# An attention and mixture-of-depths kernel: loads of k, q and v issued later, and row sums begun one turn later

## The chip, the cores and the metric

The kernel runs on one core of a Trainium2 chip. The metric is the device time of one execution in microseconds (us); of several runs of a kernel the median is given. The profile shows one execution. Its engines are PE (TensorE; PEld is its weight load), DVE (VectorE), ACT (ScalarE), POOL (GpSimd) and SP (SyncE, which here only issues transfers). "L370" is line 370 of the kernel before.

## The reference

q, k and v are 8 batches x 8 heads x 576 positions x 64, phi is 8 x 8 x 576 x 32.

```python
a = exp(phi - max(phi, axis=2)); a = a / (sum(a, axis=2) + 1e-9)   # over the 576 positions
k_m = einsum('bhsm,bhsd->bhmd', a, k)
v_m = einsum('bhsm,bhsd->bhmd', a, v)
attn = softmax(q @ k_m.T / 8)                                     # over the 32 columns
x = (attn @ v_m) with the heads side by side                      # 8 x 576 x 512
scores = x @ w_gate
for each batch: of the 128 positions with the highest scores
    out = x + sigmoid(score) * (relu(x @ w1) @ w2)                # w1 512 x 1024
all other positions: out = x
```

## The kernel before

The sequence of the work is written by hand: the kernel is a set of Python generators, and a main loop takes some steps of each in every **turn**. What a generator issues between two of its `yield`s stands together in the programs of the engines, and each engine then runs its own program in that order.

**Softmax groups.** `softmaxes` works on 16 groups (a batch and half of its heads, 128 rows by 576). A group takes eleven turns; its arithmetic is on DVE and ACT (L192 to L275; L275 is the last DVE step, in which e is finished). For the first eight groups two channels are used in alternation, for groups 8 to 15 one. `group` loads the next group's phi (L98) and its own k (L102). At its end `keys` transposes e on PE (L315), copies it with ACT (L317), splits it into a high and a low part on DVE (L321, L323), stores these parts in DRAM through POOL (`aparts`, L326), and multiplies with k on PE (L332), from which ACT makes `kbd` (L337). k has one buffer in each channel, phi has two.

**v.** `split_v` runs in every second turn while both channels live: it loads v (L284, two buffers), splits it on DVE (L294, L296) and stores both parts in DRAM through POOL (`vparts`, L299). A buffer can be loaded again when its store has landed.

**Sums.** `values` sums a x v for a set of two batches (four groups). Rows of `vparts` and `aparts` come back in 32 chunks: SP issues one transfer of 288 KB (L349) and four of 36 KB (L356) for a chunk, two chunks ahead, into three buffers, so that a load waits until PE has read the chunk three before it. PE multiplies a chunk with 72 small matmuls (L370), with a yield after each eighth. `all_sums` starts a set when its four groups are made and five more turns have passed; `steps()` says how many steps of the sums a turn takes (7 while softmaxes and `split_v` run, 10 while attentions run beside softmaxes, 12 later).

**Attention.** Two batches are worked on at a time. `attention` runs `centre` (means of k_m and v_m, L391 to L448), `scores` (q x k_m on PE, L471, then ACT and DVE, L460), then loads q of the next batch in two transfers (L106, two buffers), then `attend` (denominators L516, L521; products L527, L529; L533 and the gate scores L501 to L506 on DVE; stores through POOL), `rank` (transposes L564, comparisons L580 and L582) and `gather` (L601 and an indirect load).

**The feed-forward part.** `ffns` takes two steps in every turn when positions were chosen: transposes L624, matmuls L635 and L645, L650 on DVE, an indirect store L652.

All loads of phi, k, v, q, and of the rows are issued by SP, one after the other in the order of its program. One that waits for its buffer keeps those behind it from being issued.

Of the kernel before, what the change touches and what calls it, by code (L numbers as in the profile page):

```python
# [37 lines left out]
def kernel(  # L38
# [17 lines left out]
    B, S, D = out.shape  # L56
# [39 lines left out]
    def load_phi(i, ch):  # L96
        phis[i] = exs[ch].tile([P, S], F32, name="ph", bufs=2)
        nc.sync.dma_start(out=phis[i], in_=phiT[groups[i]])  # L98

    def load_k(i, ch):  # L100
        ks[i] = exs[ch].tile([PT, NC, D // NG], F32, name="kb")
        nc.sync.dma_start(out=ks[i], in_=k[groups[i]])  # L102

    def load_q(b, j):
        qs[b, j] = step.tile([P, NPR, S // 2], F32, name="qb")
        nc.sync.dma_start(out=qs[b, j], in_=qT[b, :, :, j * (S // 2):(j + 1) * (S // 2)])  # L106

    groups = [(b, g) for b in range(B) for g in range(NG)]
# [73 lines left out]
    def softmax(i, ch):  # L182
# [3 lines left out]
        def t(name, dtype=F32):  # L186

            return ex.tile([P, NC * P if name in WIDE else S], dtype, name=name)[:, :S]
# [27 lines left out]
        def fma(val, h, c):  # L216


            lo, big, low = t("lo"), t("big"), t("low")
            stt(out=lo, in0=val, scalar=GRID, in1=h, op0=ALU.mult, op1=ALU.subtract)  # L220
            tt(out=lo, in0=lo, in1=rh, op=ALU.mult)  # L221
            tt(out=big, in0=h, in1=rh, op=ALU.mult)  # L222
            tt(out=low, in0=val, in1=rl, op=ALU.mult)  # L223
            tt(out=low, in0=low, in1=lo, op=ALU.add)  # L224
            stt(out=val, in0=big, scalar=c * UP, in1=low, op0=ALU.add, op1=ALU.add)  # L225

        yield
        fma(den, dh, EXP_Q[0])
        dh = t("dh", I16)
        act(dh, den, GRID / 2)  # L230
# [49 lines left out]
    def split_v():  # L280

        def load(b, g):
            vb = vio.tile([P, 4 * S * Dh // P], F32, name="vb")
            nc.sync.dma_start(out=vb, in_=v[b, g])  # L284
            return vb

        coming = load(*groups[0])
        for i, (b, g) in enumerate(groups):
            vb = coming
            if i + 1 < len(groups):  # L290
                coming = load(*groups[i + 1])
            yield
            hi = vio.tile([P, 4 * S * Dh // P], F32, name="vhi")
            nc.vector.tensor_single_scalar(hi.bitcast(I32), vb.bitcast(I32), -4096,  # L294
                                           op=ALU.bitwise_and)
            nc.vector.tensor_sub(vb, vb, hi)  # L296
            yield
            for vp, src in enumerate((vb, hi)):
                nc.gpsimd.dma_start(  # L299
                    out=vparts[b, g, :, vp].rearrange("w r s d -> w (r s d)")  # L300
                                           .rearrange("w (p x) -> p w x", p=P),
                    in_=src.unsqueeze(1).to_broadcast([P, 2, 4 * S * Dh // P]))
            yield

    v_m = {}
# [249 lines left out]
    def rank(b):  # L555

        tg = tgs[b % 3]
        row = one.tile([P, S], F32, name="row")
        for c0 in range(0, NT, 4):
            cc = range(c0, min(c0 + 4, NT))  # L560
            ps = bank([P, 4 * P])
            for c in cc:
                n = tiles[c]
                nc.tensor.transpose(out=ps[:, (c - c0) * P:(c - c0) * P + n],  # L564
                                    in_=tg[:n, c, 1:2].to_broadcast([n, P]),
                                    identity=ident[:n, :n])
            n = sum(tiles[c] for c in cc)
            nc.scalar.activation(row[:, c0 * P:c0 * P + n], ps[:, :n], AF.Copy)  # L568
        yield

        less = work.tile([P, NT], F32, name="less")
        equal = work.tile([P, NT], F32, name="equal")
        sign = one.tile([P, S], BF16, name="sign")
        cmp = one.tile([P, S], BF16, name="cmp")
        for c in range(NT):
            g = tg[:, c, 1:2]
            off = (NT - 1 - c) * P
            nc.scalar.activation(sign, row, AF.Sign, bias=g, scale=-1.0,  # L580
                                 accum_out=less[:, c:c + 1])
            nc.vector.scalar_tensor_tensor(  # L582
                out=cmp, in0=row, scalar=g, in1=wide[:, off:off + S],
                op0=ALU.is_equal, op1=ALU.mult, accum_out=equal[:, c:c + 1])
            if c % 2:
                yield
        yield
        nc.vector.scalar_tensor_tensor(out=less, in0=less, scalar=-0.5, in1=equal,
                                       op0=ALU.mult, op1=ALU.add)
        st[b, "rank"] = less  # L590

    def gather(b, t):
        r0, r1 = ranks[t]
        n = r1 - r0
        pick = one.tile([P, NT, P], F32, name="pick")
        nc.vector.tensor_tensor(
            out=pick[:, :, :n], in0=iota_r[:, r0:r1].unsqueeze(1).to_broadcast([P, NT, n]),
            in1=st[b, "rank"].unsqueeze(2).to_broadcast([P, NT, n]), op=ALU.is_equal)
        ps = bank([P, 2])
        for c in range(NT):  # L600
            nc.tensor.matmul(out=ps[:n], lhsT=pick[:tiles[c], c, :n], rhs=tgs[b % 3][:tiles[c], c],  # L601
                             start=(c == 0), stop=(c == NT - 1))
        yield
        idx = work.tile([P, 1], I32, name="idx", bufs=3)
        nc.vector.tensor_copy(idx[:n], ps[:n, 0:1])
        at = work.tile([P, 1], I32, name="at", bufs=3)

        gr = work.tile([P, 1], F32, name="gr", bufs=3)
        nc.scalar.activation(gr[:n], ps[:n, 1:2], AF.Tanh, scale=0.5)
        xe = work.tile([P, D], F32, name="xe", bufs=3)  # L610
        nc.gpsimd.indirect_dma_start(
            out=xe[:n], out_offset=None, in_=xs[b],
            in_offset=bass.IndirectOffsetOnAxis(ap=idx[:n, 0:1], axis=0))
        nc.vector.tensor_scalar_add(at[:n], ps[:n, 0:1], float(b * S))
        st[b, t, "xe"] = at, xe, gr
# [41 lines left out]
    def attention(b, general=False):  # L657
        yield from centre(b)
        yield
        yield from (scores_less_max if general else scores)(b)  # L660
        if not general and b + 1 < B:
            for j in range(2):
                load_q(b + 1, j)
        yield
        yield from attend(b, general)
        yield
        yield from rank(b)
        for t in range(nt):
            yield from gather(b, t)
            chosen.append((b, t))  # L670
# [19 lines left out]
    def group(i, ch):  # L690
        at = order[ch].index(i)
        if at + 1 < len(order[ch]):
            load_phi(order[ch][at + 1], ch)
        load_k(i, ch)
        yield from softmax(i, ch)
        made.append(i)

    def softmaxes():

        todo, live, since = [list(o) for o in order], {}, 6  # L700
        while any(todo) or live:
            for ch in range(2):
                if ch not in live and todo[ch] and since >= 6:
                    live[ch] = group(todo[ch].pop(0), ch)
                    since = 0
            since += 1
            for ch in list(live):
                if next(live[ch], live) is live:
                    del live[ch]
                yield  # L710

    def steps():

        return 12 if not working else 10 if attend_all else 7

    def all_sums():
        for st in range(B // SET):
            while not all(i in made for i in range(st * SET * NG, (st + 1) * SET * NG)):
                yield
            for _ in range(5 * steps()):  # L720
                yield
            yield from values(st)
            summed.update(range(st * SET, (st + 1) * SET))
        sums_end.close()
        more.append(ctx.enter_context(tc.tile_pool(name="more", bufs=4, space=PSUM,
                                                   reuse_waits="tile")))
# [15 lines left out]
    w1_sb = weights.tile([P, KD, F], F32, name="w1_sb")  # L742
    w2_sb = weights.tile([P, KF, D], F32, name="w2_sb")
    working = [softmaxes(), split_v()]
    parts, sums, attend_all, products = None, all_sums(), None, ffns()
    turn = 0
    while True:
# [40 lines left out]
    with tc.If(taken > 0):  # L788
        for b in range(B):
            finish(attention(b, True))  # L790
            while chosen:
                finish(ffn(*chosen.pop(0)))
# [34 lines left out]
```

## Time and profile before

| | us |
|---|---|
| median of three runs | 1061.32 (1061.14 to 1063.09) |
| the profiled execution's own time | 1064.27 |
| its span in the profile | 1062.3 |
| DVE busy | 785.5 |
| PE busy | 612.8 |
| ACT busy | 293.9 |
| POOL busy | 225.6 |
| PE waiting for `a_rows` before L370 | 119.5 |

Busy time is counted within the span. A row of a timeline gives the start (us from the span's start), the duration, engine, line, operation, output<-input with shapes and how many instructions are merged in it; in square brackets stands how long the engine had been idle before it and what ended that. A row of the waits gives who waited for whom, the sum in us, how often, and the longest. Where a matmul of 32-bit numbers is merged, the profile counts two for each one of the program. The stages in time: up to about 187 us softmaxes and v alone, then the first set's sums beside them, from about 350 us softmaxes, sums and attentions together, from 806 us (the last group's transposes) attentions, feed-forward and the last set's sums, from 951 us attentions and feed-forward of the last two batches.

### The profile page before, as it was taken

What the parts mean: (1) busy time and instruction counts of PE and PEld (TensorE: products, weight loads), DVE (VectorE), ACT (ScalarE), POOL (GpSimd) and SP (SyncE); (2) the same over time, 40 slices, a digit from 0 to 9 for tenths busy, and PEclk for the clock granted to TensorE, in tenths of its full rate; (3) what the DMA queues carried; (4) which work ended last, traced back from release to release, by engine and by line L of the source; (5) the groups of instructions that cost most, each with busy time, mean ns of one, the idle gap of its engine ahead of it and who ended that gap; (6) DMA issues with size and microseconds to landing.
All of it is one profiled execution on the core that took longest, in us unless ns stands there. A gap on an engine that the chain in (4) does not pass through costs nothing.

```text
span 1062.3 us, 25397 instructions
## 1 busy us (share of the span) xinstructions
PE 612.8 (58%) x10738; PEld 451.9 (43%) x10738; DVE 785.5 (74%) x1342; ACT 293.9 (28%) x578; POOL 225.6 (21%) x335
## 2 busy tenths in 40 slices
PE   0022022253664366676747778578637867889795
PEld 0022022243564355555624555455424656554542
DVE  7899999899899869687797858868796425324940
ACT  2233133133233242312325232141442120213330
POOL 7030230220230320413214041221312101011110
PEclk9999999985655556765678788668868867899788
DMA  4773454678787644644513455373303565531320
GB/s 141 272 259 136 160 173 181 211 252 268 256 286 264 217 101 139 203 152 128 180 40 101 120 143 152 123 234 97 93 21 93 156 186 166 167 106 57 128 70 23
DMA packets 60713, 166.11 MB, mean 156 GB/s; under 512 B 10800, under 2 KB 21040, under 8 KB 60592
## 3 DMA queue, kind: packets, MB, share of 16 engines
q1 hardware_dynamic: 39088, 94.14, 29.3%
q0 software_dynamic: 21504, 70.27, 20.1%
q8 instruction: 87, 1.43, 0.6%
q14 instruction: 34, 0.28, 0.1%
HBM read 96.21 MB, written 68.16 MB: 155 GB/s over the span
## 4 chain that ended last, share of the span: by engine, by line
DVE 47%; PE 26%; DMA 9%; SPq 8%; ACT 5%; issue 4%; DVEq 0%; POOL 0%; ACTq 0%
DMA a_rows<-aparts 6%; SPq L356 6%; PE acc L370 6%; PE bank L332 4%; DVE lo L220 4%; PE bank L645 4%; DVE low L224 4%; PE bank L635 3%; DVE big L222 3%; DVE low L223 3%; DVE lo L221 3%; DVE num L225 3%; PE bank L529 3%; DVE e L274 2%; DMA v_rows<-vparts 2%
## 5 line engine op out<-in xcount | busy, mean ns | idle before, releaser
L370 PE MATMUL acc<-a_rows,v_rows 32*64 32x128 f32 x9216 | 224.7, 263 | 135.3 <-DMA a_rows<-aparts 119.5
L370 PEld LDWEIGHTS acc<-a_rows,v_rows 32*64 32x64 f32 x9216 | 204.3, 172 | 179.5 <-issue 109.0
L315 PE MATMUL bank<-ident,e 128*96 128x128 f32 x96 | 23.3, 414 | 212.8 <-DVE e L275 201.5
L315 PEld LDWEIGHTS bank<-ident,e 128*96 128x96 f32 x96 | 16.5, 190 | 219.0 <-issue 175.5
L635 PE MATMUL bank<-w_sb,xeT 128*128 128x512 f32 x128 | 69.8, 681 | 7.8 <-ACT xeT L626 6.4
L332 PE MATMUL bank<-lo,kb 96*128 96x64 f32 x384 | 69.0, 361 | 6.9 <-ACT lo L317 6.9
L326 POOL DMA_DIRECT2D aparts<-low x64 | 47.2, 745 | 119.9 <-DVE low L323 119.8
L332 PEld LDWEIGHTS bank<-lo,kb 96*128 96x128 f32 x384 | 67.1, 273 | 10.7 <-ACT lo L317 8.6
L645 PE MATMUL bank<-w_sb,hT 128*128 128x512 f32 x128 | 62.3, 622 | 0.0
L529 PE MATMUL bank<-vbd,eT 128*128 128x256 f32 x160 | 61.2, 519 | 0.0
L533 DVE TENSOR_TENSOR xj<-bank,rd 128x512 f32<-128x512 f32 x40 | 27.6, 689 | 42.4 <-PE bank L529 41.9
L176 ACT ACTIVATE vh<-num 128x576 int16<-128x576 f32 x32 | 21.8, 682 | 115.0 <-DVE num L225 113.3
L536 POOL TENSOR_TENSOR xj<-xj,mean 128x1024 f32<-128x1024 f32 (+1 forms) x12 | 26.0, 2166 | 128.6 <-DVE xj L533 118.3
L221 DVE TENSOR_TENSOR lo<-lo,rh 128x576 f32<-128x576 f32 x64 | 50.5, 790 | 2.2
L299 POOL DMA_DIRECT2D vparts<-vb x16 | 11.7, 728 | 186.2 <-DVE vb L296 161.9
L582 DVE SCALAR_TENSOR_TENSOR cmp<-row,tg,wide 128x576 bf16<-128x576 f32 x40 | 32.5, 812 | 24.9 <-ACT row L568 24.1
L220 DVE SCALAR_TENSOR_TENSOR lo<-num,vh 128x576 f32<-128x576 f32 x48 | 40.4, 842 | 13.5 <-ACT vh L176 13.5
L224 DVE TENSOR_TENSOR low<-low,lo 128x576 f32<-128x576 f32 x64 | 48.5, 758 | 2.2
L326 POOL DMA_DIRECT2D aparts<-big x64 | 47.0, 743 | 0.0
L529 PEld LDWEIGHTS bank<-vbd,eT 128*128 128x128 f32 x160 | 35.8, 248 | 17.3 <-issue 12.9
L635 PEld LDWEIGHTS bank<-w_sb,xeT 128*128 128x128 f32 x128 | 25.3, 215 | 34.5 <-issue 21.7
L176 ACT ACTIVATE low<-big,c 128x576 f32<-128x576 f32 x16 | 12.4, 775 | 99.3 <-DVE big L246 99.3
(150 smaller groups left out, 1246.8 us busy)
## 6 DMA issues: line engine op xcount, KB each, us to landing
v_rows<-vparts SPq DMA_DIRECT2D x128, 288.0 KB
vparts<-vb POOLq DMA_DIRECT2D x16, 1152.0 KB, 5.0
vparts<-vhi POOLq DMA_DIRECT2D x16, 1152.0 KB, 7.8
a_rows<-aparts SPq DMA_DIRECT2D x512, 36.0 KB
kb<-in_k SPq DMA_DIRECT2D x16, 576.0 KB
vb<-in_v SPq DMA_DIRECT2D x16, 576.0 KB
qb<-in_qT SPq DMA_DIRECT2D x16, 576.0 KB
out<-xj POOLq DMA_DIRECT2D x16, 512.0 KB, 3.9
```

What stands on the lines that cost most here:

```text
L176: nc.scalar.activation(dst, src, func, bias=biases[c] if c else 0.0, scale=s)
L220: stt(out=lo, in0=val, scalar=GRID, in1=h, op0=ALU.mult, op1=ALU.subtract)
L221: tt(out=lo, in0=lo, in1=rh, op=ALU.mult)
L224: tt(out=low, in0=low, in1=lo, op=ALU.add)
L315: nc.tensor.transpose(out=tp[:, c], in_=a[:, (c0 + c) * PT:(c0 + c + 1) * PT], identity=ident)
L326: nc.gpsimd.dma_start(out=aparts[h, b, g, part].rearrange("(c p) m -> p c m", p=PT), in_=src[:, :, h * M:(h + 1) * M])
L332: nc.tensor.matmul(out=km[:, rr], lhsT=kb[:, c, rr * P:(rr + 1) * P], rhs=aS[:, c, rr * 2 * M:(rr + 1) * 2 * M], start=(c == 0), stop=(c = ...
L356: nc.sync.dma_start(out=a_rows[ch % 3][2 * h::8, h].rearrange("p s m -> p (s m)").bitcast(F32), in_=src.unsqueeze(1).to_broadcast([4 * SET ...
L370: nc.tensor.matmul(out=accs[i][:Dh, :P].rearrange("p (h m) -> p h m", m=M), lhsT=vr[p, s], rhs=ar[p, :, s], start=(ch == 0 and s == 0), st ...
L529: nc.tensor.matmul(out=o[:, g * 4 * Dh:(g + 1) * 4 * Dh], lhsT=eT[:, g, (c0 + c) * P:(c0 + c + 1) * P], rhs=vbd[b % 3][:, g], start=False, ...
L635: nc.tensor.matmul(out=ps[:n], lhsT=xeT[:, d, :n], rhs=w1_sb[:, d, f0:f0 + 512], start=(d == 0), stop=(d == KD - 1))
L645: nc.tensor.matmul(out=ps[:n], lhsT=hT[:, f, :n], rhs=w2_sb[:, f], start=(f == 0), stop=(f == KF - 1))
```

## The change

The load of k moves from the start of a group to the fourth of its steps, after three yields. The load of the next v moves from before the splitting of the present one to behind its store. The two loads of the next q are issued in two turns instead of one, which gives every attention one yield more. The sums of a set start after six more turns instead of five. No operation is added or taken away.

```diff
@@ softmax
         yield
+        load_k(i, ch)
         fma(den, dh, EXP_Q[0])
@@ split_v
             vb = coming
-            if i + 1 < len(groups):
-                coming = load(*groups[i + 1])
             yield
...
                     in_=src.unsqueeze(1).to_broadcast([P, 2, 4 * S * Dh // P]))
+            if i + 1 < len(groups):
+                coming = load(*groups[i + 1])
             yield
@@ attention
         yield from (scores_less_max if general else scores)(b)
-        if not general and b + 1 < B:
-            for j in range(2):
+        for j in range(2):
+            yield
+            if not general and b + 1 < B:
                 load_q(b + 1, j)
-        yield
         yield from attend(b, general)
@@ group
             load_phi(order[ch][at + 1], ch)
-        load_k(i, ch)
         yield from softmax(i, ch)
@@ all_sums
-            for _ in range(5 * steps()):
+            for _ in range(6 * steps()):
                 yield
```

## The prediction

> **What bounds the kernel now.** I read the page first, then busy time by stage, then SP's own waits, then the timelines of DVE and PE around the places where DVE stands still.
>
> ```profile
> PE 612.8 (58%) x10738; PEld 451.9 (43%) x10738; DVE 785.5 (74%) x1342; ACT 293.9 (28%) x578; POOL 225.6 (21%) x335
> L370 PE MATMUL acc<-a_rows,v_rows 32*64 32x128 f32 x9216 | 224.7, 263 | 135.3 <-DMA a_rows<-aparts 119.5
> ```
>
> DVE is the busiest, but the mean hides stages, so I cut the span where the work changes: the softmaxes alone (to 350 us), softmaxes with attentions (to 806, where the last group's transposes start), the last set's sums (824 to 951), the tail.
>
> ```profile
> 0.00:350.00 350.00, 108.58 (x2416) 100.00 (x2416) 318.03 (x466) 101.53 (x161) 84.99 (x142) 0.86 0.66 220
> 350.00:806.00 456.00, 296.22 (x5454) 219.92 (x5453) 362.58 (x645) 139.96 (x289) 105.85 (x134) 0.71 0.44 129
> 824.00:951.00 127.00, 102.83 (x2493) 75.18 (x2493) 43.97 (x85) 18.00 (x45) 11.47 (x18) 0.83 0.53 161
> 951.00:1062.30 111.30, 88.58 (x305) 47.11 (x303) 52.76 (x123) 29.61 (x72) 16.46 (x30) 0.85 0.21 68
> ```
>
> The columns after the length are PE, PEld, DVE, ACT, POOL. DVE is 91% busy up to 350 and its gaps there are 0.75 to 0.85 us waits for ACT: DVE alone sets that stage. From 350 to 806 DVE works 363 of 456 us; the 93 us between are what a better order can win. After 806 PE is at 80% or more and sets the end, together with SP, which needs 0.50 + 2.45 + gaps = 3.09 us to issue the five DMAs of one row chunk: 32 chunks are 99 of that stage's 127 us.
>
> Now the waits that the change aims at, SP's own:
>
> ```profile
> SPq L284 <- DMA vparts<-vb: 166.8, 10, 25.6
> SPq L349 <- PE acc L370: 136.4, 46, 19.9
> SPq L102 <- PE bank L332: 77.0, 5, 45.0
> SPq L106 <- PE bank L471: 60.9, 3, 35.0
> ```
>
> They look large and mostly cost nothing. In SP's timeline the v waits (L284) lie almost all before 187 us, when no row load has been issued yet; behind them stand only phi and k loads that are needed tens of us later. Two delay rows, by 5 us (to 212.6) and 8 us (to 238.4), in the stage that DVE sets. The longest k wait ends at 569.7, but the rows behind it need the group's aparts, which land at 575.5. The longest q waits end at 817.4, and the last aparts land at 818.
>
> What costs is where PE stands in DVE's way. After each group's last DVE step (L275) PE, which waited at L315, has to do everything it was held up from at once:
>
> ```profile
> 682.52 1.48 PE L315 MATMUL bank<-ident,e 128*96 128x128 f32 x6 [12.01 <-DVE e L275]
> 683.93 2.40 PE L370 MATMUL acc<-a_rows,v_rows 32*64 32x128 f32 x80
> 686.26 5.38 PE L332 MATMUL bank<-lo,kb 96*128 96x64 f32 x24
> 691.58 2.40 PE L370 MATMUL acc<-a_rows,v_rows 32*64 32x128 f32 x80
> 693.90 1.17 PE L564 MATMUL bank<-ident,tg 128*128 128x128 f32 x5
> 695.66 0.82 DVE L582 SCALAR_TENSOR_TENSOR cmp<-row,tg,wide 128x576 bf16<-128x576 f32 x1 [6.22 <-ACT row L568]
> ```
>
> DVE loses 6.22 us here because its next work (L582) needs a transpose that lies behind 11.7 us of PE work. Summing DVE's gaps of this sort in the 35 us after each L275: group 8 8.7, 9 11.4, 10 10.5, 11 6.8, 12 10.6, 13 10.4, 14 6.3: 64.7 of the 93 us. Some of them are rows that came late:
>
> ```profile
> 442.37 0.38 SPq L98 DMA_DIRECT2D ph<-in_phiT  x1
> 442.79 0.43 SPq L102 DMA_DIRECT2D kb<-in_k  x1
> 445.13 6.67 DMA a_rows<-aparts
> 452.83 1.97 PE L370 MATMUL acc<-a_rows,v_rows 32*64 32x128 f32 x64 [6.00 <-DMA a_rows<-aparts]
> ```
>
> phi and k (288 + 576 KB) were issued just ahead; the rows then took 6.67 us to land, where others of this kernel take 1.0, PE waited 6.0 us and DVE 2.28.
>
> **What the Trainium skill says.** "Perfetto Trace Analysis", section "DMA Instruction — HWDGE (DVE, Sync)": an SP row starts when its semaphores are satisfied and ends when the sequencer is free; moving the data is not in it. The trace agrees: rows of 0.4 us for 576 KB, and a landing of 6.67 us after the last. "DMA: Bandwidth & Descriptors", "Queues, rings and completion order": each DMA engine takes descriptors in ring order, so a big load issued first delays the rows wherever SP itself stands; 6.67 against 1.0 us agrees. "TensorE: Matmul & The Clock Gate", "What's actually happening": PE falls to half clock after idling and needs some us of work to leave it. The same 24 L332 rows take 5.38 us at 686 and 2.6 to 2.8 us elsewhere. It adds that the point of the switch varies between runs of one kernel, so I can't say which groups will be slow.
>
> **The change, part by part.** I counted both programs' order on each engine and the turns of the main loop.
>
> *k three turns later, v after the store, q one load per turn.* No transfer and no instruction is added. In the first stage: worth nothing, DVE covers it (cover gone: the 5 and 8 us above, at most). v is now issued four turns (about 15 us at 350 us for 92 turns) instead of six before its use; a landing even as late as the worst one above (6.67 us) fits. k has six turns, q three (about 15 us); both fit. No wait is added: v still waits for the store of two groups back, now issued six turns earlier (23 us) instead of two, and k and rows queue behind it on SP as before. POOL's stores and DVE's splitting of v keep their places. In the second stage k no longer goes out together with phi in the burst after L275. Of late rows DVE lost 2.28 (457), about 2.4 (523 to 525), 1.75 and 1.09 us (702, 706): 7.5 us. Bounds 0 and 7.5; I take 2, because 576 KB still pass, later, with rows two chunks ahead.
>
> *Sums one turn later (6 instead of 5), attention one turn longer (the second yield in its loop over j).* This moves work against the groups: the first chunks of the four sets go from turns 53, 98, 137, 180 to 54, 100, 138, 181, attention 0's attend from 108 to 110, 1's from 120 to 122, 2's from 142 to 145, 3's from 154 to 157, while the groups' transposes stay at turns 98, 109, 120, 131, 142, 153, 164, 175. DVE's own work up to L275 of the last group changes by 0.4 us only. What changes is what lies between L315 and DVE's next need. By hand, group 9 of before: DVE has 0.4 us to do, then waits 1.8 for L321; L533 needs L315 1.5 + L370 2.4 + L527/L529 2.7 = 6.6 us, a gap of 2.9; the next L533 needs 5.5 more of PE, gap 4.2; sum 8.9 (and 0.8 for L200) against 9.1 in the trace, so the method holds. With the order after: group 8 7.0, 9 7.8, 10 5.2, 11 4.0, 12 8.0, 13 5.2, 14 5.8 = 43.0 with PE at full clock when it comes to L332 (group 8 apart). In before three of the seven groups (8, 10, 13) had L332 slow; a slow one costs 2.6 (L332) + 0.9 (80 L370) + 1.2 (L527/L529) = 4.7 us, so two more add 9.4: 52.4. Groups 9, 11 and 12 gain because centre work now fills DVE while it waits for L321, group 13 because L533 and not L564 comes next. 64.7 - 52.4 = 12 us. The hand count leaves out rows that come late in the burst; I take 7 off the span besides the 2 above. Bounds: -20 (all groups fast, no late rows) to +5 (three more slow ones, and late rows in each burst).
>
> *What is late next.* PE work is pushed behind the last group. After its L315, PE has 4 L624 rows (0.65 us) and two steps of L635 (1.9 each) more than before: 4.4 us. Of it -1.1 before the sums begin (ffn steps replace attend 4's first matmuls), +3.5 within the sums (L516, L527, L529 of one pass and one L645 step), +1.9 in the tail (an L645 step that used to be done by 951). PE waits 24 us for rows within the sums, in ten waits of 0.3 to 4.7 us, which hide part of the 3.5; I take 2, sum about +4, bounds 0 and +9 (a turn there is 127/24 = 5.3 us, if all is stretched).
>
> *Sum.* -2 - 7 + 4 = -5: a span of 1057.3 instead of 1062.3. The profiled execution took 1064.27, 2.0 around its span; the median of the runs is 1061.32. The same 5 off it: **1056**.
>
> **Rivals.** *Slower (0.30)*: DVE's gaps only move from group to group, since PE must do the same work after each L315, and the pushed work is paid: 1061 + 4 to 8 = 1067. It decides from the point where the gaps of groups 8 to 14 still sum to over 60 us. For it: total work is unchanged and PE sets the last 240 us. Against: the fillers. *No change (0.15)*: the loads waited with nothing behind them (all of SP's long waits above), the gain and the +4 cancel: 1061, within 2. *A large gain (0.15)*: late rows vanish as well and PE meets the groups at full clock: 20 off, 4 back, 1045. *Forecast (0.40)*: 1050 to 1059.
>
> **How the numbers follow.** 0.2% (2.1 us) is about what a measurement of this kernel can tell from no change. Faster: forecast and large gain, 0.55; same 0.15; slower 0.30. Leaving out a tenth at each end, past the middle of the large gain and of the slower case: 1043 to 1070; the forecast's own range is 1050 to 1059.
>
> **What would show it.** Right: DVE busy unchanged near 785, the last L315 at about 798 instead of 806.7, gaps after L275 of groups 8 to 14 summing to some 50 to 58; SP's wait for vparts far below 166.8 with the first stage still ending near 350; the sums from L315 of the last group to the last L370 about 2 us longer than 144, the tail about 2 longer. Wrong: the last L315 at 806 or later, or v landing after its L294 needs it (a DVE wait on v, of which there is none now), or rows of the last set starving PE for much more than 24 us.

## The result, and the profile after

| | before | after |
|---|---|---|
| median, us | 1061.98 (1061.14 to 1063.09, 4 runs) | 1054.0 (1051.72 to 1054.93, 4 runs) |
| the profiled execution's own time | 1064.27 | 1053.18 |
| its span | 1062.3 | 1051.3 |
| start of the last group's transposes | 806.66 | 790.75 |

The ratio is 0.9921 (0.99 to 0.9942): 8 us faster, against 5 predicted. Ratios here and below are taken round by round and leave disturbed executions out, so they are not exactly quotients of medians.

Between k's new place (L228) and q's loads, the kernel after has each line one higher than before, and so have the experiments that move k: L370 is L371, L315 is L316, L332 is L333, and so on. The page of the kernel after, engines and the sums' matmuls:

```profile
PE 598.7 (57%) x10738; PEld 439.8 (42%) x10738; DVE 784.4 (75%) x1342; ACT 293.6 (28%) x578; POOL 224.3 (21%) x335
L371 PE MATMUL acc<-a_rows,v_rows 32*64 32x128 f32 x9216 | 217.8, 257 | 106.7 <-DMA a_rows<-aparts 97.6
```

DVE does the same work. PE's wait for rows fell from 119.5 to 97.6 us, and PE's own time by 14 us for the same instructions, which fits a higher clock (0.805 over the span against 0.792). Stretches of the kernel after (columns: stretch, its length, then PE, PEld, DVE, ACT and POOL busy with their instructions, PE's clock, DMA share, GB/s):

```profile
0.00:350.00 350.00, 107.77 (x2472) 99.31 (x2472) 317.97 (x466) 101.98 (x163) 84.93 (x142) 0.87 0.66 219
350.00:790.00 440.00, 277.38 (x5382) 207.17 (x5384) 360.65 (x642) 137.48 (x283) 103.58 (x133) 0.73 0.44 133
790.75:814.80 24.05, 19.33 (x70) 12.11 (x68) 7.34 (x24) 6.41 (x17) 8.03 (x14) 0.68 0.44 119
814.80:936.40 121.60, 102.98 (x2506) 73.07 (x2505) 44.08 (x85) 17.73 (x42) 11.31 (x17) 0.87 0.54 168
936.40:1051.30 114.90, 90.49 (x313) 48.12 (x310) 53.78 (x125) 29.91 (x73) 16.49 (x30) 0.84 0.20 66
```

The kernel before, between the same events (last group's transposes, first and last row matmul of the last set):

```profile
806.66:824.30 17.64, 16.92 (x79) 9.73 (x79) 7.58 (x25) 4.85 (x12) 7.01 (x13) 0.90 0.47 115
824.30:950.70 126.40, 102.23 (x2491) 74.84 (x2490) 43.69 (x84) 17.77 (x43) 11.28 (x17) 0.82 0.53 161
950.70:1062.30 111.60, 88.89 (x310) 47.41 (x306) 52.96 (x124) 29.83 (x73) 16.46 (x30) 0.85 0.21 68
```

So the sum of the difference is -15.9 up to the last group's transposes, +6.4 from there to the last set's first rows, -4.8 within its sums and +3.3 in the tail: -11.0, the difference of the spans. In the first stage DVE is as busy as before, and group 8's transposes come at 377.2 us instead of 378.2: nearly all of the 15.9 lies between group 8 and the last group.

The gaps of DVE there, summed much as in the prediction (0.9 us or more, in the 36 us after each L315), us:

| group | 8 | 9 | 10 | 11 | 12 | 13 | 14 | sum |
|---|---|---|---|---|---|---|---|---|
| before | 7.9 | 10.5 | 10.0 | 6.8 | 12.3 | 10.4 | 6.3 | 64.2 |
| after | 7.8 | 7.6 | 8.0 | 7.4 | 7.8 | 11.3 | 2.4 | 52.3 |

SP's own waits after (who waited for whom, sum, times, longest):

```profile
SPq L350 <- PE acc L371: 159.9, 46, 23.3
SPq L285 <- DMA vparts<-vb: 153.9, 8, 28.2
...
SPq L102 <- PE bank L431: 37.9, 1, 37.9
...
SPq L102 <- PE bank L333: 5.2, 2, 2.7
```

The wait of v's loads (L285) is still there, 153.9 of 166.8 us. k's loads wait 43.1 us in two rows (37.9 and 5.2) where they waited 77.0. The 37.9 is one wait that ends at 557.8 us, put down to L431; it is the load that in the kernel before waited 45.0 for L332 until 569.7, so that one has hardly changed. What has gone are the shorter waits.

So far this fits the prediction's account, in which the later sums bring the gain and the loads almost none. The experiments say otherwise.

### The profile page after: what moved, and what is told of

The parts are those of the page before. It is cut to its first block, busy times and chain, and to the rows that moved or that the text cites. A ratio compares the mean times of both kernels' runs of the same rounds, so it can differ in the third digit from the quotient of the medians.

```text
span 1051.3 us, 25384 instructions
## 1 busy us (share of the span) xinstructions
PE 598.7 (57%) x10738; PEld 439.8 (42%) x10738; DVE 784.4 (75%) x1342; ACT 293.6 (28%) x578; POOL 224.3 (21%) x335
## 5 line engine op out<-in xcount | busy, mean ns | idle before, releaser
L371 PE MATMUL acc<-a_rows,v_rows 32*64 32x128 f32 x9216 | 217.8, 257 | 106.7 <-DMA a_rows<-aparts 97.6
L371 PEld LDWEIGHTS acc<-a_rows,v_rows 32*64 32x64 f32 x9216 | 197.7, 167 | 150.2 <-issue 113.9
L316 PE MATMUL bank<-ident,e 128*96 128x128 f32 x96 | 22.5, 403 | 214.8 <-DVE e L276 204.6
L316 PEld LDWEIGHTS bank<-ident,e 128*96 128x96 f32 x96 | 16.0, 185 | 219.7 <-issue 183.4
L333 PE MATMUL bank<-lo,kb 96*128 96x64 f32 x384 | 67.0, 353 | 7.6 <-ACT lo L318 6.8
L333 PEld LDWEIGHTS bank<-lo,kb 96*128 96x128 f32 x384 | 65.5, 267 | 12.1 <-ACT lo L318 8.6
L646 PE MATMUL bank<-w_sb,hT 128*128 128x512 f32 x128 | 67.2, 661 | 0.0
L636 PE MATMUL bank<-w_sb,xeT 128*128 128x512 f32 x128 | 65.5, 647 | 2.9 <-ACT xeT L627 2.9
L221 DVE TENSOR_TENSOR lo<-lo,rh 128x576 f32<-128x576 f32 x64 | 56.7, 885 | 2.2
L220 DVE SCALAR_TENSOR_TENSOR lo<-num,vh 128x576 f32<-128x576 f32 x48 | 36.0, 751 | 13.2 <-ACT vh L176 13.2
L602 PE MATMUL bank<-tg,pick 128*128 128x2 f32 (+1 forms) x80 | 16.9, 329 | 47.4 <-DVE pick L597 20.2
```

The lines of the kernel that those rows point to most:

```text
L316: nc.tensor.transpose(out=tp[:, c], in_=a[:, (c0 + c) * PT:(c0 + c + 1) * PT], identity=ident)
L333: nc.tensor.matmul(out=km[:, rr], lhsT=kb[:, c, rr * P:(rr + 1) * P], rhs=aS[:, c, rr * 2 * M:(rr + 1) * 2 * M], start=(c == 0), stop=(c = ...
L371: nc.tensor.matmul(out=accs[i][:Dh, :P].rearrange("p (h m) -> p h m", m=M), lhsT=vr[p, s], rhs=ar[p, :, s], start=(ch == 0 and s == 0), st ...
L636: nc.tensor.matmul(out=ps[:n], lhsT=xeT[:, d, :n], rhs=w1_sb[:, d, f0:f0 + 512], start=(d == 0), stop=(d == KD - 1))
L646: nc.tensor.matmul(out=ps[:n], lhsT=hT[:, f, :n], rhs=w2_sb[:, f], start=(f == 0), stop=(f == KF - 1))
```

## The experiments

Each ratio is to the kernel before on the same chip: its median was 1063.98 us beside the first four kernels (22 executions), 1062.27 beside the next four (49) and 1064.45 beside the last four (11).

### The three loads alone

k and v as in the change, q's two loads around the one yield that was there; sums after five turns.

```diff
@@ softmax
         yield
+        load_k(i, ch)
@@ group
-        load_k(i, ch)
@@ split_v
-            if i + 1 < len(groups):
-                coming = load(*groups[i + 1])
...
+            if i + 1 < len(groups):
+                coming = load(*groups[i + 1])
@@ attention
-        if not general and b + 1 < B:
-            for j in range(2):
-                load_q(b + 1, j)
+        if not general and b + 1 < B:
+            load_q(b + 1, 0)
         yield
+        if not general and b + 1 < B:
+            load_q(b + 1, 1)
```

> Only the loads are moved: k after three yields, v after its store, the two q loads in two turns around the one yield that attention has in the kernel before; sums after five turns. Shift theory (the gain comes from sums and attentions standing at other turns against the softmax groups, loads are worth nothing): 1061 to 1063, ratio 0.998 to 1.002, last L315 at 805 to 808 us. Load theory (row loads no longer stand behind k, q and v): nearly the whole gain, 1053 to 1056, last L315 near 791.

Measured: 1057.46 us (1055.6 to 1061.9), ratio 0.9938 (0.9912 to 0.9963). Some 6.6 us, between what the two theories had expected, above the 2 that the prediction took and within its bound of 7.5. In its profile (of the slowest of its eight executions) SP still waits 64.0 us for k's buffer, 40.9 of it in the one long wait near 560 us that the kernel before has too.

### The order alone

Six turns and the second yield, all loads as before.

```diff
         yield
+        yield
         yield from attend(b, general)
...
-            for _ in range(5 * steps()):
+            for _ in range(6 * steps()):
```

> Only the order: sums after six turns and one yield more in attention; k, v and q loaded where the kernel before loads them. Shift theory: nearly the whole gain, 1053 to 1057, DVE's gaps before the last L315 near 91 us as with the whole change (105 before). Load theory: no gain before the last group and PE work pushed behind it, so 1063 to 1068.

Measured: 1072.59 us (1068.0 to 1078.94), ratio 1.009 (1.0057 to 1.0124): **slower** by 0.9%, where the prediction's two terms for the order, -7 and +4, give -3 us. The order alone isn't where the gain is. Its time can be laid beside that of other kernels stage by stage, each from one profiled execution (us; that of the order alone took 1076.45, 3.9 above its median, that of the loads alone 1061.9):

| kernel | last group's transposes at | from there to the last set's first rows | its sums | tail | span |
|---|---|---|---|---|---|
| before | 806.7 | 17.6 | 126.4 | 111.6 | 1062.3 |
| loads alone | 801.6 | 17.6 | 130.9 | 110.0 | 1060.1 |
| order alone | 804.5 | 24.1 | 131.3 | 114.8 | 1074.7 |
| after | 790.8 | 24.1 | 121.6 | 114.9 | 1051.3 |
| six turns alone (below) | 803.7 | 18.9 | 119.4 | 110.2 | 1052.2 |
| loads and six turns (below) | 792.0 | 19.2 | 114.2 | 111.8 | 1037.2 |

The order alone is slower than the kernel before because of what it pushes behind the last group: +6.5, +4.9 and +3.2, 14.6 us. Up to the last group it wins 2.1. But group 8's transposes come 4.0 us earlier (374.2 instead of 378.2), and there two profiles of one and the same program, the kernel after, also differ by 2.9 us. From group 8 on it loses 1.8; DVE's gaps of groups 8 to 14 sum to 70.2 us instead of 64.2. Against the kernel after it is 13.8 us later at the last group. Two places make up 13.4 of the 17.9 us by which its gaps there are longer.

The first is group 8. The timeline of the order alone, SP, then PE, then DVE (lines as in the kernel before):

```profile
344.53 0.63 SPq L98 DMA_DIRECT2D ph<-in_phiT  x1
381.64 0.34 SPq L102 DMA_DIRECT2D kb<-in_k  x1
382.04 0.48 SPq L349 DMA_DIRECT2D v_rows<-vparts  x1
...
389.14 1.34 PE L370 MATMUL acc<-a_rows,v_rows 32*64 32x128 f32 x40 [7.02 <-DMA a_rows<-aparts]
...
392.43 0.46 DVE L460 SCALAR_TENSOR_TENSOR eT<-es,th 128x288 f32<-128x288 f32 x1 [4.68 <-ACT th L458]
```

SP stands for 36 us between phi and k. The view of SP's waits of the same kernel has it (sum, times, longest):

```profile
SPq L102 <- PE bank L332: 49.6, 5, 36.4
```

k of group 9 needs the buffer that group 8 gives free only at its L332, near 381 us. In the kernel before, SP and then DVE at the same place, the first rows of the second set go out ahead of that load:

```profile
353.58 0.65 SPq L349 DMA_DIRECT2D v_rows<-vparts  x1
...
391.42 0.43 SPq L102 DMA_DIRECT2D kb<-in_k  x1
...
390.44 0.46 DVE L460 SCALAR_TENSOR_TENSOR eT<-es,th 128x288 f32<-128x288 f32 x1 [1.50 <-ACT th L458]
```

With six turns they stand behind it: the rows of the set's first chunks are issued at 382 us, PE, which has done group 8's matmuls by then, waits 7.02 us for them, and DVE, whose L460 lies behind, 4.68. The kernel after, the same engines at the same place:

```profile
348.61 0.64 SPq L98 DMA_DIRECT2D ph<-in_phiT  x1
349.63 0.48 SPq L350 DMA_DIRECT2D v_rows<-vparts  x1
...
395.31 0.44 SPq L102 DMA_DIRECT2D kb<-in_k  x1
...
385.02 1.34 PE L371 MATMUL acc<-a_rows,v_rows 32*64 32x128 f32 x40
...
391.21 0.46 DVE L461 SCALAR_TENSOR_TENSOR eT<-es,th 128x288 f32<-128x288 f32 x1 [0.50 <-ACT th L459]
```

The rows go out at 349.6, k at 395.3, when its buffer has been read. PE finds its rows there and DVE waits 0.50. DVE's gaps after group 8 sum to 12.5 us in the order alone, 7.9 before and 7.8 after.

The second place is group 12, where the order alone puts two loads of q, one of phi and one of k (2 x 576 + 288 + 576 = 2016 KB) directly ahead of rows. The timeline of the order alone, SP, PE and DVE:

```profile
625.97 1.36 SPq L106 DMA_DIRECT2D qb<-in_qT  x2
627.44 1.28 SPq L98 DMA_DIRECT2D ph<-in_phiT  x1
628.76 0.90 SPq L102 DMA_DIRECT2D kb<-in_k  x1
629.76 0.48 SPq L349 DMA_DIRECT2D v_rows<-vparts  x1
...
640.63 2.19 PE L370 MATMUL acc<-a_rows,v_rows 32*64 32x128 f32 x72 [6.71 <-DMA a_rows<-aparts]
...
645.27 0.69 DVE L533 TENSOR_TENSOR xj<-bank,rd 128x512 f32<-128x512 f32 x1 [9.12 <-PE bank L529]
```

After, SP issues phi at 620.83, q at 625.39 and 630.23 and k at 634.07, and PE's and DVE's timelines read:

```profile
636.60 0.34 PE L371 MATMUL acc<-a_rows,v_rows 32*64 32x128 f32 x8 [1.88 <-DMA a_rows<-aparts]
...
638.23 0.69 DVE L534 TENSOR_TENSOR xj<-bank,rd 128x512 f32<-128x512 f32 x1 [1.90 <-PE bank L530]
```

PE waits 1.88 instead of 6.71, DVE 1.90 instead of 9.12; group 12's gaps sum to 7.8 instead of 16.5.

### Six turns alone, and the second yield alone

```diff
-            for _ in range(5 * steps()):
+            for _ in range(6 * steps()):
```

> Only the sums after six turns instead of five. Shift theory: a part of the gain, as attentions start with the sums and so move by a turn or two, but their later turns move one less: 1054 to 1062, not slower than 1064. Load theory: slower by what is pushed behind the last group, 1062 to 1066.

```diff
         yield
+        yield
         yield from attend(b, general)
```

> Only the second yield in attention (both q loads before it). Shift theory: attend, rank and gather stand a turn later against the groups, a part of the gain of about the size of the rest, 1054 to 1062. Load theory: no gain, and a turn more behind the last group, 1062 to 1066.

Measured: six turns 1053.29 us (1052.24 to 1061.19), ratio 0.9923 (0.9897 to 0.9949); the yield 1066.93 (1053.83 to 1071.37), ratio 1.0026 (1.0 to 1.0052). Together, above, they are 0.9% slower, though one alone gains 0.8% and the other loses 0.3% (0 to 0.5): the parts don't add. The six turns alone already show the harm at group 8 (gaps of 12.6 us, a k wait of 34.2), and their gain doesn't lie in DVE's gaps, which sum to 109.6 us up to the last group against 104.7 before. It lies in large part behind the last group: the last row matmul comes 138.3 us after the last group's transposes instead of 144.1, and the tail is 110.2 instead of 111.6. Why the sums are shorter there isn't shown; PE's clock in them is 0.87 instead of 0.82. The yield's profiled execution was the fastest of its twelve, so only the length of its tail is used, further below.

### The order with one load each

To find which load repairs the order, it ran with k's move, with q's split (one load in each of the two turns) and with v's move, in this order:

```diff
@@ softmax
         yield
+        load_k(i, ch)
@@ group
-        load_k(i, ch)
```

> The order of the whole change (six turns, second yield) with k moved, v and q loaded as in the kernel before. Late-row theory (with six turns, set 1's first rows stand behind the k load of group 9, which waits 36 us for L332; and k goes out in one burst with phi and both q): the gaps after group 8's L315 fall from 12.5 to about 8 us, part of the burst at group 12 goes, 1060 to 1067 (order alone 1072.6). Shift theory: no difference, 1070 to 1075.

```diff
@@ attention
-        if not general and b + 1 < B:
-            for j in range(2):
+        for j in range(2):
+            yield
+            if not general and b + 1 < B:
                 load_q(b + 1, j)
-        yield
```

> The order of the whole change with the q loads in two turns, k and v as in the kernel before. Late-row theory: group 8's 12.5 us of gaps stay (k still stands before the rows), group 12's 16.5 shrink, 1064 to 1070. Shift theory: 1070 to 1075.

```diff
@@ split_v
-            if i + 1 < len(groups):
-                coming = load(*groups[i + 1])
...
+            if i + 1 < len(groups):
+                coming = load(*groups[i + 1])
```

> The order of the whole change with v moved, k and q as in the kernel before. Late-row theory and the prediction: v's waits lie in the stage that DVE alone sets, so no difference from order alone: 1070 to 1075. If instead v is the part that held rows back: 1055 to 1064.

| kernel | median, us | ratio | gaps after group 8, us |
|---|---|---|---|
| order alone | 1072.59 | 1.009 (1.0057 to 1.0124) | 12.5 |
| order and k | 1055.54 (1047.45 to 1064.6) | 0.992 (0.9892 to 0.9948) | 7.8 |
| order and q | 1066.87 (1061.15 to 1074.5) | 1.0039 (1.002 to 1.0059) | 12.7 |
| order and v | 1072.31 (1064.44 to 1082.42) | 1.0078 (1.0053 to 1.0102) | 12.9 |

k's move is worth 1.7%, some 18 us, and only it brings the gaps after group 8 back to those of the kernel before. (Its profile is of the second slowest of its fifteen executions, 1064.1 us; even so its gaps of groups 8 to 14 sum to 58.8 us, where the order alone has 70.2.) How the 18 us are spread over the stages this profile can't tell. q's split is worth about 0.5%, 5 us, at intervals that just overlap, with group 12's gaps at 11.4 instead of 16.5. v's move changes nothing that the intervals can tell, as predicted.

### The loads and six turns, with one yield

The three loads as in the first experiment (v's part and the old place of k's load aren't shown again), and six turns.

```diff
@@ softmax
         yield
+        load_k(i, ch)
@@ attention
-            for j in range(2):
-                load_q(b + 1, j)
+            load_q(b + 1, 0)
         yield
+        if not general and b + 1 < B:
+            load_q(b + 1, 1)
         yield from attend(b, general)
@@ all_sums
-            for _ in range(5 * steps()):
+            for _ in range(6 * steps()):
```

> Loads moved and sums after six turns, but attention keeps one yield (the two q loads stand on either side of it). If the second yield only costs (alone it gave 1.0026) and the other two parts add up (0.9938 and 0.9923 alone): ratio about 0.986, some 1048 us, faster than the whole change. If the second yield is what makes the other two work together: 0.992 or worse, 1054 or more.

Measured: **1039.64 us** (1034.07 to 1041.2), ratio 0.9767 (0.9731 to 0.9803): 2.3% faster than before, and faster than the kernel after, whose ratios (0.9921 above, 0.9872 below) lie outside its interval. The two gains alone, 0.9938 and 0.9923, would have added up to 0.986.

### The whole change again, beside the second yield in two halves

The change as it is ran once more in the last batch.

> The whole change again, beside the next three on one chip. 0.992 of the kernel before, as before; the version with the loads and six turns but one yield (e5) gave 0.9767.

Measured: 1053.09 us (1046.44 to 1057.72), ratio 0.9872 (0.9828 to 0.9916). Against the 0.9767 without the second yield that yield costs about 1%, 11 us; with the first measurement's 0.9921, 16.

Where? The timeline of the kernel after at the last group, PE and then DVE:

```profile
790.75 1.52 PE L316 MATMUL bank<-ident,e 128*96 128x128 f32 x6
795.96 1.09 PE L625 MATMUL bank<-ident,xe 128*128 128x128 f32 x4 [3.69 <-DVE kbd L394]
796.84 5.22 PE L333 MATMUL bank<-lo,kb 96*128 96x64 f32 x24
...
804.06 0.46 DVE L461 SCALAR_TENSOR_TENSOR eT<-es,th 128x288 f32<-128x288 f32 x1 [8.18 <-ACT th L459]
```

The profile names kbd, which DVE finishes at 795.89 us; the rows that `gather` fetches (issued at 790.87, 5.0 us to landing) land at the same moment. The second run of the same program tells the two apart: there DVE finishes kbd at 798.14, after PE has started, so what PE waits for are the rows. Its PE timeline:

```profile
798.10 1.08 PE L625 MATMUL bank<-ident,xe 128*128 128x128 f32 x4 [3.57 <-DMA xe<-xs,idx]
```

With one yield, the wait falls ahead of the group's transposes, when PE has nothing else that is due. PE's timeline of the loads and six turns with one yield:

```profile
791.16 1.08 PE L625 MATMUL bank<-ident,xe 128*128 128x128 f32 x4 [5.13 <-DMA xe<-xs,idx]
792.04 1.48 PE L316 MATMUL bank<-ident,e 128*96 128x128 f32 x6
...
796.30 2.79 PE L333 MATMUL bank<-lo,kb 96*128 96x64 f32 x24
```

The same 24 matmuls take 5.22 us there and 2.79 here. The wait of 3.69 didn't slow PE down: in both kernels it was slow already (L316 takes 1.52 and 1.48 us, where in the kernel after group 14's six take 0.82). The difference is what PE does between the end of the wait and L333: 0.9 us of work there, 5.1 here. The Trainium skill states what fits this ("TensorE: Matmul & The Clock Gate", section "What's actually happening": PE's clock is halved by default and after idling, and is released by some us of work); the durations agree, and the granted clock from the last group to the first rows is 0.68 against 0.90 with one yield. That stretch takes 24.0 to 24.1 us in all six profiles with six turns and the full second yield, 18.9 and 19.2 in the two with six turns and one yield: 5 us that repeat.

That made the early attentions the suspect, since gather of batch 3 is what meets the last group. Two kernels keep the second yield for half of the batches only, on top of the loads and six turns:

```diff
+        if b < 2 * SET:          # early: batches 0 to 3
+            yield
         if not general and b + 1 < B:
             load_q(b + 1, 0)
...
```

> As e5 (loads moved, six turns), with a second yield in the attentions of batches 0 to 3 only. Theory: the second yield costs mainly because it puts gather of batch 3, and with it the transposes L624 that need the gathered rows, behind L315 of the last group, where PE then waits about 3.7 us for the gathered rows and falls to half clock before L332: from the last L315 to the first L370 24 us instead of 19, and 1046 to 1053 us, 0.985 to 0.992. Rival (the cost lies in the attentions of the last batches, which are stretched in the sums of the last set and in the tail): 0.977 to 0.980 as without any second yield.

```diff
+        if b >= 2 * SET:         # late: batches 4 to 7
+            yield
...
```

> As e5, with a second yield in the attentions of batches 4 to 7 only. Theory: the transposes stay before L315, 19 us to the first L370; only the pushed work of the tail (one L645 step, some 2 to 3 us) and one pass of L516 to L529 in the sums are paid: 1040 to 1046, 0.978 to 0.984. Rival: most of the 1.5%, 0.988 to 0.992.

Measured: early 1043.56 us (1035.97 to 1056.3), ratio 0.9782 (0.9736 to 0.9829); late 1047.81 (1047.15 to 1049.07), 0.9834 (0.9799 to 0.9869). Late lies in the range that the suspicion gave it, early below its range. So the suspect isn't the costly one: with the early yield the kernel is as fast as without any, within the intervals, although its profile (of its slowest execution, 1056.3 us) has the same wait, 3.71 us, and 26.8 us from the last group to the last set's first rows; with the late yield these are 16.7. More of the cost seems to go with the late attentions. Busy time of two stretches shows what they do, the sums and the tail, in the kernel with the late yield:

```profile
804.62:931.30 126.68, 106.64 (x2502) 75.98 (x2501) 43.95 (x85) 17.13 (x41) 11.32 (x17) 0.84 0.54 166
931.30:1046.20 114.90, 90.51 (x314) 48.26 (x310) 53.77 (x125) 29.90 (x73) 16.53 (x30) 0.84 0.20 66
```

The same stretches in the kernel with one yield:

```profile
811.20:925.40 114.20, 98.08 (x2493) 70.22 (x2492) 43.45 (x84) 17.14 (x41) 11.30 (x17) 0.90 0.57 179
925.40:1037.20 111.80, 88.84 (x310) 47.41 (x306) 53.42 (x124) 29.80 (x73) 16.47 (x30) 0.84 0.20 68
```

The tail is 3.1 us longer. This repeats: 112.6 to 115.0 us in the seven other profiles with a late second yield, 110.0 to 112.0 in the five other profiles without one. The sums' 12.5 us differ with PE's clock, 0.84 against 0.90, with 9 more matmuls only (2502 against 2493). They vary widely between kernels that have the same late yield (121.6 us after, 126.7 here, 131.3 with the order alone). Yet no profile with six or seven turns and without the late yield is as long: these four have 113.0 to 119.4, the seven with six turns and the late yield 121.6 to 131.3. So the late yield probably lengthens the sums too; by what way isn't shown. The intervals of late, early and whole overlap at their ends: that the late half carries most of the cost is likely, not settled.

### Seven turns

The loads with one yield, sums after seven turns instead of six.

```diff
-            for _ in range(6 * steps()):
+            for _ in range(7 * steps()):
```

> As e5 with seven turns before the sums. Shift theory: the places of attention against the groups move again, the gain is no trend: between 0.977 and 0.995, and the work pushed behind the last group costs 2 to 5 us, so not faster than e5. If starting the sums later is good in itself: 0.965 to 0.975.

Measured: 1048.34 us (1039.1 to 1053.23), ratio 0.9819 (0.977 to 0.9869), about half a per cent slower than with six, at intervals that overlap. So a start later still brings no further gain; why, this run alone doesn't show.

## Why the prediction was right, and where it was not

**Right in time, and in where it shows.** 1054.0 was measured and 1056 predicted. DVE's busy time stayed (784.4; "near 785"), the first stage is about as long, the gaps of groups 8 to 14 sum to 52.3 us where the hand count gave 52.4, the sums from the last transposes to the last row matmul are 1.6 us longer (2 were forecast). The last transposes came at 790.8 us, not "about 798": with 7 taken of the counted 12 and 2 for late rows, -9 was forecast before the last group, and -15.9 came.

**In part luck.** Group by group the count is off: group 13's gaps were to be 5.2 us and are 11.3, group 14's 5.8 and are 2.4. In the second profile of the same program the seven sum to 58.7. Its second measurement, 0.9872, would be 1048 us on the forecast's base, below its 1050. And as the stages show, errors of both signs behind the last group made up the +4 (below).

**The step that failed: "This moves work against the groups ... I take 7 off the span besides the 2".** It gave the gain to the order and 2 us to the loads. With the order alone the last transposes come 2.1 us earlier (1.8 later, counted from group 8) and 14.6 us are added behind them; it is 0.9% slower. The loads, given the order, are worth 1.7 to 2.2% (from 1.009 to 0.992 and 0.987). The hand count was made with the order after, and left late rows out of it; that they would not be late was due to the loads. So the 12 us were both parts' together, booked on one. The same error stands in the loads' step. It priced k's waits by what stood behind them in before ("the rows behind it need the group's aparts", true there) and said of the changed program only that k and rows queue behind v "as before". With six turns the second set's first rows move from turn 98 to 100, behind a k load that waits 36.4 us. The prediction had the rows' turns, and did not lay SP's program of the order alone beside them.

**"Bounds 0 and 7.5; I take 2"** for the loads in the old order: 6.6 us measured, within the bounds, at their upper end. The price of a late row was read too high, though: 6.67 us stands beside 1.0 "of others", but of the 17 waits for rows on that profile's chain of work that ended last 13 take more than 3 us, four of them in the last set, where no k, v or phi is loaded. **v "worth nothing"**: held, 1.0078 against 1.009. But "SP's wait for vparts far below 166.8" did not: 153.9. Six turns of head start changed that wait little, and it costs nothing, as it lies in the stage that DVE sets.

**The +4 behind the last group** came as +4.9 (+6.4, -4.8, +3.3), but not as booked. Its own terms, -1.1, +2 and +1.9, sum to 2.8 and not to 4. The -1.1 ahead of the sums was +6.4: the term took the pushed L625 rows for 0.65 us of work and not for matmuls that wait for gathered rows, 3.69 us, and leave PE at half clock for L333. Within the sums +2 was -4.8, and the tail's +1.9 was +3.3. The first and the last repeat in the other kernels with the full second yield; the -4.8 does not (the order alone has +4.9 there).

**The rivals.** "Gaps only move" (1067) fell at its own mark: 52.3, and 58.7 in the second profile, under 60. The order alone, with 70.2 us of gaps and 1072.6 us, is what comes nearest to that rival. The large gain, 1045 by late rows vanishing and PE at full clock, is what the same change without its second yield reaches and passes: 1039.64.

**Open.** Of the 11 to 16 us that the second yield costs, 5 (to the first rows) and 3 (tail) repeat; the rest stands in the sums, +7.4 us between the profiles of the kernel after and of its form with one yield, and by what way isn't shown. Nor is it how the early yield can pay those 5 and hardly be slower, or how the spread between executions arises (below).

## What to carry to other kernels

A load that waits at the head of SP's queue cost here by what stood behind it, and that was decided by the order after the change: before moving work by a turn, write down the issuing engine's own program around each waiting load, once with the move alone. Move such loads to where their buffer is free first, then the work: the same order lost 0.9% with the loads in their old places and gained 0.8 to 1.3% with them moved. The parts of this schedule didn't add, so run each one alone and each one left out; and follow work that is pushed behind the last stage, for the order lost its 14.6 us there.

## What the runs showed of the hardware

One program's executions spread widely on one chip: 1053.83 to 1071.37 us for the second yield alone, 1055.99 to 1070.28 for the kernel before in the second batch, while the late yield stayed within 1047.15 to 1049.07. The stretch of the last sums goes broadly with PE's clock: 0.90 at 114.2 us, 0.87 at 121.6, 0.84 at 126.7, 0.82 at 126.4 and 131.3, 0.79 at 130.9; but 0.86 at 113.0 with seven turns. Whether small waits decide how much of the time PE runs at half clock, and so the spread, was not isolated.
